# Ninety-five of 174 tensor subtractions of a transformer block go from the vector engine to GpSimd

## The chip, the core and the metric

The kernel runs on one core of a Trainium2 chip. The core's engines run side by side, each through its own fixed queue of instructions: PE multiplies matrices, DVE does element-wise work and reductions, ACT does activations and casts, POOL is GpSimd, and SP issues the DMAs. An instruction waits only for semaphores of instructions that it depends on. The metric is the device time of one execution in microseconds (us); the median of three runs of the kernel before is 856.67 us (856.55 to 857.07).

## The reference

One pre-norm transformer block in float32 on 2048 tokens of width 640. Attention is local and dilated: each token sees itself and the 7 tokens at distances 2, 4, ... 14 before it, in 32 heads of width 20. The feed-forward part is a SwiGLU of width 1728.

```python
def _A_ref(x, wqkv, wo):          # H=32, Dh=20, W=8, dil=2
    idx = pos[:, None] - (arange(W) * dil)[None, :]
    logits = einsum("bhsd,bhswd->bhsw", q, kg) * Dh ** -0.5
    logits = where(idx >= 0, logits, -1e9)
    o = einsum("bhsw,bhswd->bhsd", softmax(logits, -1), vg)
    return o.reshape(B, S, D) @ wo
def _B_ref(x, w_gate, w_up, w_down):
    return (silu(x @ w_gate) * (x @ w_up)) @ w_down
h = x + _A_ref(layernorm(x), A_wqkv, A_wo)
h2 = h + _B_ref(layernorm(h), B_w_gate, B_w_up, B_w_down)
```

## The kernel before

**High and low halves.** PE multiplies a rounded format (fp32r) at one pass. To keep float32 accuracy, every operand is split: ACT casts it to fp32r (the high half), DVE subtracts that from the float32 value (the low half), and PE makes three passes: high by high, low by high, high by low. So each weight tile, each layer-norm output, each attention output and each gated activation costs one cast on ACT and one subtraction on DVE. The sites of these subtractions are L438 (turned layer-norm columns), L508 (Q, K and V weights), L669 (output weights), L714 (attention output), L788 (feed-forward weights) and L842 (gated activations).

**Stages.** The tokens go in four blocks of 512 (b = 0 to 3), the heads in four groups of eight (g). L536 makes Q, K and V of a block and group in 15 matmuls per bank; ACT evicts them (L543) and SP writes them to DRAM. Attention has no matmul: for each of the 16 pairs (b, g), DVE multiplies Q with the windows of K (L600, two halves of 2560 elements a partition), sums over the 20 channels (L605), takes the maximum over the 8 keys and subtracts it (L616, L617); ACT takes the exponential (L618); DVE sums, inverts and scales (L624 to L626), multiplies with V (L631), adds the eight keys in three steps (L640) and transposes (L647). SP stores the result (L653). When all four groups of a block have stored one half, SP loads it as columns (L709), ACT and DVE split it (L713, L714), and PE multiplies with the output weights (L724; for the last block L1054). Then follow layer norm and 14 feed-forward tiles: gate and up (L812), silu on ACT (L847), the product on DVE (L848), its split (L841, L842), and down (L827, L977). L392 and L481 are transposes of layer-norm output on PE, and L395 and L396 split what they give. The feed-forward weights of block 0 are split and saved (L803), and blocks 1 and 2 load most of them back (L798).

**Order.** Nothing is scheduled on the chip. Every step is registered with its engine, its reads and its writes (`P.add`), and `ORDER`, a table of numbers written into the kernel, says for each engine in which order its steps are emitted. PE, DVE, ACT and SP work through that order, and a step that is late holds up all that stand behind it on its engine. In the kernel before, POOL has only memsets and the making of an identity matrix. The costs that `P.add` is given play no part on the chip.

Of the kernel before, what the change touches and what calls it, by code (L numbers as in the profile page):

```python
# [8 lines left out]
F32 = mybir.dt.float32  # L9
# [17 lines left out]
QUEUES = (0, 1) * 8  # L27
TURN1, TURN2 = (2,), (2,3)
# [141 lines left out]


def dve(n):
    return 0.155 + 0.00104 * n


tt = dve


def nb(chunks, size):
    return (chunks / 16 * 0.042 + chunks * size / 435e3) * RATE  # L180


# [4 lines left out]
def program(tc, x_in, wqkv_in, wo_in, ffn_in, ffl_in, const_in, out):  # L187
    nc = tc.nc
    V, A, T, Q, G = nc.vector, nc.scalar, nc.tensor, nc.sync, nc.gpsimd
    P = Plan()  # L190
# [1092 lines left out]
```

## Time and profile before

| | |
|---|---|
| median of three runs | 856.67 us (856.55 to 857.07) |
| profiled execution, its own time | 859.16 us |
| its span | 857.4 us |
| PE busy | 845.8 us (99%), 3977 matmuls |
| DVE busy | 696.7 us (81%), 807 instructions |
| ACT busy | 412.3 us (48%), 722 instructions |
| POOL busy | 3.3 us, 12 instructions |
| DMA moved | 177.75 MB, mean 207 GB/s |
| granted clock of PE, mean | 0.998 |

The page's busy tenths show DVE at nine tenths or more from the third of 40 slices to the twenty-eighth (one of them at eight), about 43 to 600 us: attention runs there from about 60 us on. PE is busy all through, because the feed-forward work of one block is interleaved with the attention of the next. The busy time of PE hides gaps of up to some 0.16 us between matmuls, since a matmul is shown longer (390 ns for 512 columns) than the distance to the next one (227 ns, 20.40 us for 90 of them in the chain of waits).

### The profile page before, as it was taken

How to read it: one execution, taken by the hardware profiler on the slowest of the kernel's cores; microseconds unless marked ns; L12 is line 12 of the kernel's file. 1: busy time of each engine (PE TensorE's matmuls, PEld its weight loads, DVE VectorE, ACT ScalarE, POOL GpSimd, SP SyncE). 2: the span in 40 equal slices, each digit the busy share in tenths (PEclk: the TensorE clock that was granted, in tenths of full speed). 3: DMA queues.
4: the chain of work that ended last, by engine and by line, in shares of the span. 5: the costliest groups of instructions: out<-in, count | busy, mean ns of one | idle time of the engine just before them, and what ended most of it. 6: DMA issues, size and time to landing. Idle time of an engine off the chain costs nothing.

```text
span 857.4 us, 10685 instructions
## 1 busy us (share of the span) xinstructions
PE 845.8 (99%) x3977; PEld 718.0 (84%) x3977; DVE 696.7 (81%) x807; ACT 412.3 (48%) x722; POOL 3.3 (0%) x12
## 2 busy tenths in 40 slices
PE   7999999999989999999999999999999999999998
PEld 6888888889978888888888888778888888888886
DVE  5499999999999999998999999999666865553333
ACT  6766555342783434576343458454356423232332
POOL 0000000000000000000000000000000000000000
PEclk9999999999999999999999999999999999999999
DMA  5997795779798889648989987887653213362312
GB/s 185 277 262 180 231 280 137 210 200 239 218 266 269 278 271 278 215 118 293 318 269 285 306 263 200 246 305 274 251 172 101 98 53 99 97 216 100 107 31 93
DMA packets 86852, 177.75 MB, mean 207 GB/s; under 512 B 33408, under 2 KB 51584, under 8 KB 86032
## 3 DMA queue, kind: packets, MB, share of 16 engines
q1 hardware_dynamic: 85392, 176.41, 67.2%
q10 hardware_dynamic: 1408, 0.66, 0.3%
q8 instruction: 31, 0.51, 0.2%
q14 instruction: 21, 0.17, 0.1%
HBM read 132.07 MB, written 43.65 MB: 205 GB/s over the span
## 4 chain that ended last, share of the span: by engine, by line
PE 97%; ACT 1%; DVE 1%; DMA 1%; issue 0%; SPq 0%; ACTq 0%; DVEq 0%
PE bank L812 35%; PE bank L536 24%; PE bank L827 21%; PE bank L977 7%; PE bank L724 6%; PE bank L1054 2%; PE bank L392 1%; DMA fa<-in_x_dram 1%; PE bank L481 0%; PE bank L1161 0%; ACT L847 0%; ACT L618 0%; ACT ra L793 0%; ACT shb L395 0%; DVE fa L352 0%
## 5 line engine op out<-in xcount | busy, mean ns | idle before, releaser
L812 PE MATMUL bank<-shb,ra 128*128 128x512 f32 x1050 | 251.8, 390 | 1.7 <-ACT shb L395 1.2
L812 PEld LDWEIGHTS bank<-shb,ra 128*128 128x128 f32 x1050 | 196.2, 188 | 43.3 <-ACT shb L395 1.4
L827 PE MATMUL bank<-ra,acts 128*128 128x512 f32 x656 | 170.4, 391 | 0.0
L827 PEld LDWEIGHTS bank<-ra,acts 128*128 128x128 f32 x656 | 122.0, 188 | 24.1
L536 PE MATMUL bank<-ra,sha 128*128 128x512 f32 (+2 forms) x480 | 108.3, 384 | 0.3 <-ACT sha L483 0.3
L536 PE MATMUL bank<-ra,shb 128*128 128x512 f32 (+1 forms) x470 | 102.7, 378 | 0.0
L536 PEld LDWEIGHTS bank<-ra,sha 128*128 128x128 f32 x480 | 90.6, 190 | 13.8 <-ACT sha L483 0.6
L536 PEld LDWEIGHTS bank<-ra,shb 128*128 128x128 f32 x470 | 88.0, 188 | 12.6
L600 DVE TENSOR_TENSOR pq<-kv,pq 128x2560 f32<-128x2560 f32 x32 | 90.2, 2820 | 2.6 <-DMA kv<-ksc 2.2
L640 DVE TENSOR_TENSOR pq<-pq 128x1280 f32<-128x1280 f32 (+2 forms) x96 | 89.7, 934 | 2.3
L631 DVE TENSOR_TENSOR pq<-kv,pq 128x2560 f32<-128x2560 f32 x32 | 90.3, 2823 | 0.9
L605 DVE TENSOR_REDUCE pq<-pq 128x128 f32<-128x2560 f32 x32 | 90.0, 2812 | 0.4
L788 DVE TENSOR_TENSOR ra<-fa,ra 128x640 fp32r<-128x640 f32 x70 | 56.3, 819 | 26.6 <-ACT ra L778 23.7
L543 ACT ACTIVATE st<-bank,fa 128x480 f32<-128x480 f32 (+3 forms) x120 | 50.6, 474 | 55.7 <-PE bank L536 41.4
L778 ACT CAST ra<-fa 128x640 fp32r<-128x640 f32 x56 | 40.6, 727 | 57.0 <-PE bank L827 56.2
L841 ACT CAST acts<-fa 128x512 fp32r<-128x512 f32 x52 | 32.1, 620 | 61.1 <-DVE fa L848 45.5
L793 ACT CAST ra<-fa 128x1280 fp32r<-128x1280 f32 (+1 forms) x41 | 50.0, 1220 | 23.5 <-PE bank L812 17.6
L724 PE MATMUL bank<-ra 128*128 128x320 f32 x360 | 56.3, 309 | 0.0
L724 PEld LDWEIGHTS bank<-ra 128*128 128x128 f32 x360 | 54.3, 188 | 1.9 <-ACT fa L727 0.5
L848 DVE TENSOR_TENSOR fa<-bank,fa 128x512 f32<-128x512 f32 x42 | 28.8, 686 | 28.7 <-PE bank L812 19.8
L847 ACT ACTIVATE fa<-bank 128x512 f32<-128x512 f32 x42 | 25.1, 597 | 55.1 <-PE bank L812 53.2
L827 PE MATMUL bank<-acts,ra 128*128 128x512 f32 x164 | 45.3, 391 | 0.1
(161 smaller groups left out, 871.5 us busy)
## 6 DMA issues: line engine op xcount, KB each, us to landing
fa<-in_ffn_dram SPq DMA_DIRECT2D x47, 960.0 KB, 6.6
kv<-ksc SPq DMA_DIRECT2D x32, 440.0 KB, 6.0
kv<-vsc SPq DMA_DIRECT2D x32, 440.0 KB, 6.8
ra<-lsc SPq DMA_DIRECT2D x21, 640.0 KB, 6.0
lsc<-ra SPq DMA_DIRECT2D x13, 640.0 KB, 6.5
ra<-lsc SPq DMA_DIRECT2D x23, 320.0 KB, 5.2
ksc<-st SPq DMA_DIRECT2D x32, 160.0 KB, 3.9
pq<-qsc SPq DMA_DIRECT2D x16, 320.0 KB, 5.6
```

The lines of the kernel that those rows point to most:

```text
L536: T.matmul(banks[bk][:, 0:n], l, r_(wq(g, w, c) + shift, n), start=(p, c) == first_mm, stop=(p, c) == last_mm)
L543: P.add("ACT", act(m) + 0.06, lambda: A.activation(stage_t()[:, o : o + NJ * m].rearrange("p (t j c) -> p t j c", j=NJ, c=w)[:, :, j, :], ...
L600: P.add("DVE", dve(2560), lambda: V.tensor_tensor(pq(PROD, 2560).rearrange("p (j w c) -> p j w c", j=2, w=W), window(ko, 2 * jp), pq(qo + ...
L605: P.add("DVE", dve(2560), lambda: V.tensor_reduce(pq(lo + 128 * jp, 128), pq(PROD, 2560).rearrange("p (n d) -> p n d", d=DH), axis=AX.X, o ...
L631: V.tensor_tensor(pq(PROD, 2560).rearrange("p (j n d) -> p j n d", j=2, d=DH), bass.AP(tensor=v.tensor, offset=v.offset, ap=[list(v.ap[0]) ...
L640: V.tensor_add(dst(v), v[:, :, 0:m, :], v[:, :, m : 2 * m, :])
L724: T.matmul(banks[bk][:, 0:320], l, r_(m, 320), start=p == 0 and c == 0, stop=p == 2 and c == NC - 1)
L788: P.add("DVE", tt(640), lambda o=o: V.tensor_sub(ws(t, lo + o, 640)[p0:], fa[p0:, raw + o : raw + o + 640], ws(t, hi + o, 640)[p0:].bitcas ...
L793: P.add("ACT", act(n), lambda: A.copy(ws(wt, gu, n), f(raw, n)), r=[rf(raw, n)], w=[rws(wt, gu, n)], prio=PR["fh"])
L812: T.matmul(banks[bk], ws(wt, gu + 1280 * w + wid * c + col, 128), x(a, c), start=p == 0 and c == 0, stop=p == 2 and c == NC - 1)
L827: T.matmul(banks[k], l, m, start=first and p == 0, stop=stop and p == len(passes) - 1)
L977: T.matmul(banks[bk], ws(wt, o + 2048 * w + 128 * k, 128), xv_[k](a), start=first and p == 0 and k == 0, stop=stop and p == 2 and k == n - ...
```

## The change

It has four parts. A helper `low` numbers the subtractions at the sites above, and those of the attention maxima (L617), in the order in which the program registers them; those whose number is in `POOLED` go to POOL, the others stay on DVE. The activations' subtractions of blocks 2 and 3 (L842) keep DVE in any case. The logits of a group are laid out by head, row and key, where they were by row, key and head, so the maximum and the sum read eight neighbours. The normalised weights are written into the buffer of the queries, in the layout that the product with V reads. And the order of all engines is a new table. A placeholder that belonged to POOL belongs to SP now; the cost figures given to `P.add` for PE and the reciprocal also differ.

```diff
+POOLED = (1, 2, 3, 7, 9, 10, 12, 14, 18, 19, ... 161, 162, 164, 166, 167, 170)
 ORDER = {
     "PE": (
-        (0, 4), 10, 5, 4, (11, 6), (25, 2), (17, 3), (27, 8), 6, (20, 2), (35, 2), ...
+        0, 9, 1, (10, 2), 5, (2, 3), 6, (12, 3), (25, 2), 8, 7, 27, (15, 7), ...
...
+def pool(n):
+    return 0.2 + 0.00218 * n
...
+        def low(n, fn, r, w, prio):
+            k = lows[0]
+            lows[0] += 1
+            if k in POOLED:
+                P.add("POOL", pool(n), lambda: fn(G), r=r, w=w, prio=prio)
+            else:
+                P.add("DVE", dve(n), lambda: fn(V), r=r, w=w, prio=prio)
...
             P.add("DVE", dve(2560), lambda: V.tensor_reduce(
-                pq(lo + 128 * jp, 128), pq(PROD, 2560).rearrange("p (n d) -> p n d", d=DH), axis=AX.X, op=ALU.add),
+                logits(lo)[:, :, 16 * jp : 16 * jp + 16].rearrange("p h n -> p n h"), pq(PROD, 2560).rearrange("p (n h d) -> p n h d", h=8, d=DH), axis=AX.X, op=ALU.add),
...
-            P.add("DVE", dve(256), lambda: V.tensor_sub(lg, lg, mx[:, :, None, :].to_broadcast([128, NJ, W, 8])), ...
+            low(256, lambda E: E.tensor_sub(groups(lo), groups(lo), each(mo)), [rpq(lo, 256), rpq(mo, 32)], [rpq(lo, 256)], 20)
...
-            P.add("DVE", dve(256), lambda: V.tensor_mul(lg, lg, sm[:, :, None, :].to_broadcast([128, NJ, W, 8])), ...
+            P.add("DVE", dve(256), lambda: V.tensor_mul(
+                pq(qo, 256).rearrange("p (j w h) -> p h j w", j=NJ, w=W), pq(lo, 256).rearrange("p (h j w) -> p h j w", j=NJ, w=W),
+                pq(mo + 32, 32).rearrange("p (h j) -> p h j", j=NJ)[:, :, :, None].to_broadcast([128, 8, NJ, W])),
...
-                P.add("DVE", tt(640), lambda o=o: V.tensor_sub(ws(t, lo + o, 640)[p0:], ...
+                low(640, lambda E, o=o: E.tensor_sub(ws(t, lo + o, 640)[p0:], ...
```

The 95 that POOL takes are, by elements of a partition: 46 of 640, 29 of 512, 7 of 480 or 448, and 13 of 256, among these the maxima of 8 of the 16 groups. No other instruction is added or removed but one activation-table load on ACT fewer (33 to 32); PE has the same matmuls.

Three places show how the order moves. The names in the rows: `ra`, `shb`, `acts` are halves for PE, `fa` holds raw float32 data, `pq` is the attention's buffer, `kv` the windows of K and V, `bank` are PSUM banks. On DVE, the last group of block 1, from the softmax's sum to the first half's transpose; before:

```order
L624 TENSOR_REDUCE pq<-pq 128x32
L625 RECIPROCAL pq<-pq 128x32
L626 TENSOR_TENSOR pq<-pq 128x256
L631 TENSOR_TENSOR pq<-kv,pq 128x2560
L848 TENSOR_TENSOR fa<-bank_75,fa 128x512
L640 TENSOR_TENSOR pq<-pq 128x2x640
L842 TENSOR_TENSOR acts<-fa,acts 128x512
L788 TENSOR_TENSOR ra<-fa,ra 128x640 x2
L640 TENSOR_TENSOR pq<-pq 128x2x320
L640 TENSOR_TENSOR pq<-pq 128x2x160
L647 STREAM_TRANSPOSE pq<-pq 128x2x5x32
```

and in the changed kernel:

```order
L640 RECIPROCAL pq<-pq 128x32
L806 TENSOR_TENSOR ra<-fa,ra 128x640
L641 TENSOR_TENSOR pq<-pq 128x8x32
L869 TENSOR_TENSOR fa<-bank_75,fa 128x512
L806 TENSOR_TENSOR ra<-fa,ra 128x640
L649 TENSOR_TENSOR pq<-kv,pq 128x2560
L658 TENSOR_TENSOR pq<-pq 128x2x640
L806 TENSOR_TENSOR ra<-fa,ra 128x640
L658 TENSOR_TENSOR pq<-pq 128x2x320
L658 TENSOR_TENSOR pq<-pq 128x2x160
L665 STREAM_TRANSPOSE pq<-pq 128x2x5x32
```

(L806 is the old L788, L869 the old L848, and so on.) Some low halves still stand between the attention's steps, but from the program's start to the first-half transpose of block 1's last group DVE now has 32 subtractions of these kinds instead of 81, to that of block 2 it has 48 instead of 126, and to that of block 3 it has 65 instead of 160.

The queue of POOL in the stretch in which block 1's attention ends, where it had nothing:

```order
L806 TENSOR_TENSOR ra<-fa,ra 128x640 x5
L861 TENSOR_TENSOR acts<-fa,acts 128x512 x2
L732 TENSOR_TENSOR ra<-fa,ra 128x512
L806 TENSOR_TENSOR ra<-fa,ra 128x640 x6
L732 TENSOR_TENSOR ra<-fa,ra 128x512 x2
L732 TENSOR_TENSOR ra<-fa,ra 128x256
L806 TENSOR_TENSOR ra<-fa,ra 128x640 x4
```

Four of block 1's six low halves of the attention output (L732, the old L714) stand here, among 17 subtractions of the feed-forward part; the two others stayed on DVE.

On PE, the end of the Q, K and V matmuls, where the feed-forward part begins; before:

```order
L392 MATMUL bank_76<-fa 128x128 x4
L392 MATMUL bank_75<-fa 128x128 x4
L392 MATMUL bank_74<-fa 128x128 x4
L536 MATMUL bank_73<-ra,shb 128x512 x15
L536 MATMUL bank_72<-ra 128x448 x5
L536 MATMUL bank_72<-ra,shb 128x448 x5
L536 MATMUL bank_72<-ra 128x448 x5
L392 MATMUL bank_76<-fa 128x128 x4
L392 MATMUL bank_75<-fa 128x128 x4
L812 MATMUL bank_74<-shb,ra 128x512 x5
```

and in the changed kernel:

```order
L546 MATMUL bank_71<-ra,shb 128x448 x15
L403 MATMUL bank_75<-fa 128x128 x4
L403 MATMUL bank_74<-fa 128x128 x4
L403 MATMUL bank_76<-fa 128x128 x4
L546 MATMUL bank_72<-ra 128x448 x5
L546 MATMUL bank_72<-ra,shb 128x448 x5
L546 MATMUL bank_72<-ra 128x448 x5
L403 MATMUL bank_75<-fa 128x128 x4
L830 MATMUL bank_74<-shb,ra 128x512 x15
```

One group of four transposes, not two, stands between the last Q, K and V matmul and the first feed-forward matmul. Further on, the first matmul with the output weights has 1573 matmuls ahead of it for block 1 before and 1502 now (71 of 512 columns fewer), 2273 and 2213 for block 2, 2730 and 2725 for block 3.

More of the change, by code (lines that the diff above doesn't have):

```diff
@@ L609, in att_exp, with groups, each @@
+        def groups(lo):
+            return pq(lo, 256).rearrange("p (n w) -> p n w", w=W)
+        def each(o):
+            return pq(o, 32)[:, :, None].to_broadcast([128, 32, W])
         def att_exp(b, g, n, ko, vo, qo, lo, mo):
[L610 removed]
             if b == 0:
                 P.add("DVE", dve(256), lambda: V.tensor_add(
[L613 removed]
+                    logits(lo), logits(lo), f(MASK, 32)[:, None, :].to_broadcast([128, 8, 32])),
@@ L841, in act_split @@
             P.add("ACT", act(512), lambda: A.copy(o(0), i()), r=[srcr], w=[("ab", ao, ao + 512)], prio=0)
-            P.add("DVE", dve(512), lambda: V.tensor_sub(o(1), i(), o(0).bitcast(F32)), r=[srcr, ("ab", ao, ao + 512)], w=[("ab", ao + 512, ao + 1024)], prio=0)
+            if b < 2:
+                low(512, lambda E: E.tensor_sub(o(1), i(), o(0).bitcast(F32)), [srcr, ("ab", ao, ao + 512)], [("ab", ao + 512, ao + 1024)], 0)
+            else:
+                P.add("DVE", dve(512), lambda: V.tensor_sub(o(1), i(), o(0).bitcast(F32)), r=[srcr, ("ab", ao, ao + 512)], w=[("ab", ao + 512, ao + 1024)], prio=0)
         def gate_up(b, i, wt, gu, ao, so, first):
@@ L1113, in wo3 @@
                     apply(j)
-            P.add("POOL", 0.02, lambda: None, w=[("fakv0", 0, KV_N), ("fakv1", 0, KV_N), ("xh", 0, 2560)] + [(f"xk{fq}", 0, 2560) for fq in range(4)], prio=0)
+            P.add("SP", 0.02, lambda: None, w=[("fakv0", 0, KV_N), ("fakv1", 0, KV_N), ("xh", 0, 2560)] + [(f"xk{fq}", 0, 2560) for fq in range(4)], prio=0)
             for n in range(16):
```

42 lines of the change are left out of this document (19 added, 23 removed), and 156 rows, old and new, of the table ORDER.

## The prediction

> **What bounds the kernel now.** I read the shares of the engines, the chain of waits, the waits of PE, then the stretch of attention by windows and by lines. The page's engine row and its chain:
>
> ```profile
> span 857.4 us, 10685 instructions
> PE 845.8 (99%) x3977; PEld 718.0 (84%) x3977; DVE 696.7 (81%) x807; ACT 412.3 (48%) x722; POOL 3.3 (0%) x12
> ...
> PE 97%; ACT 1%; DVE 1%; DMA 1%; issue 0%; SPq 0%; ACTq 0%; DVEq 0%
> ```
>
> PE carries 97% of the chain, so an edit on DVE and POOL can win only what PE waits, and can lose without limit. What PE waits for (engine and line, waited for: us in total, times, longest):
>
> ```profile
> PE bank L481 <- DVE sha L484: 2.1, 1, 2.1
> PE bank L407 <- POOL ra L1185: 1.4, 1, 1.4
> PE bank L812 <- ACT shb L395: 1.2, 1, 1.2
> PE bank L481 <- DVE fa L354: 0.9, 1, 0.9
> PE bank L392 <- DVE shb L396: 0.7, 1, 0.7
> PE bank L536 <- ACT ra L529: 0.6, 1, 0.6
> PE bank L812 <- ACT fa L847: 0.5, 1, 0.5
> PE bank L536 <- ACT sha L483: 0.3, 1, 0.3
> ```
>
> These sum to 7.7 us, all in eight single waits. The first, second, fourth and eighth belong to the start (4.7 us); 0.6, 0.7 and 1.2 us are the seam from Q, K and V to the feed-forward part. DVE is the engine that is nearly a second bound, in one stretch (us; PE, PEld, DVE, ACT, POOL busy with counts; clock, DMA share, GB/s):
>
> ```profile
> 200.00:600.00 400.00, 396.87 (x1905) 336.88 (x1904) 380.65 (x396) 204.70 (x323) 0.73 (x2) 1.00 0.84 259
> ```
>
> DVE is busy 380.65 of 400 us and idle 19.35; PE is idle 3.13. So PE's order already lives with a DVE that is 95% full. Whether the change helps hangs on what DVE's load becomes there, and on how much of the relief PE's new order has spent in advance.
>
> **The change part by part.** *What DVE gives up.* The same stretch by lines on DVE (line, operation, tiles, shapes, count | busy us, mean ns | idle before):
>
> ```profile
> L631 DVE TENSOR_TENSOR pq<-kv,pq 128x2560 f32<-128x2560 f32 x22 | 62.1, 2822 | 0.5
> L640 DVE TENSOR_TENSOR pq<-pq 128x1280 f32<-128x1280 f32 (+2 forms) x66 | 61.6, 934 | 1.5
> L600 DVE TENSOR_TENSOR pq<-kv,pq 128x2560 f32<-128x2560 f32 x21 | 59.2, 2821 | 2.5 <-DMA kv<-ksc 2.2
> L605 DVE TENSOR_REDUCE pq<-pq 128x128 f32<-128x2560 f32 x21 | 59.0, 2811 | 0.2
> L788 DVE TENSOR_TENSOR ra<-fa,ra 128x640 fp32r<-128x640 f32 (+1 forms) x41 | 32.7, 817 | 0.0
> L848 DVE TENSOR_TENSOR fa<-bank,fa 128x512 f32<-128x512 f32 x29 | 19.8, 684 | 5.3 <-PE bank L812 4.3 <-ACT fa L847 1.0
> L842 DVE TENSOR_TENSOR acts<-fa,acts 128x512 fp32r<-128x512 f32 x28 | 19.0, 677 | 1.0 <-ACT acts L841 1.0
> L714 DVE TENSOR_TENSOR ra<-fa,ra 128x512 fp32r<-128x512 f32 (+1 forms) x15 | 8.6, 594 | 0.0
> L616 DVE TENSOR_REDUCE pq<-pq 128x32 f32<-128x256 f32 x11 | 7.1, 646 | 0.2
> L624 DVE TENSOR_REDUCE pq<-pq 128x32 f32<-128x256 f32 x11 | 7.0, 640 | 1.7 <-ACT pq L618 1.7
> ```
>
> By the order, POOL's 27th to 76th subtractions (from the first feed-forward weights to the last maximum) fall in about this stretch: 25 of 640 elements, 19 of 512 and 6 of 256. On DVE they cost 25 x 0.82 + 19 x 0.68 + 6 x 0.42 = 35.9 us (the last from the row of the subtraction of the maxima, below). The 10 before that in the start replace 6.6 us in a DVE that waits for weights there, and the 19 after it stand where DVE has room (39.07 us busy of 60 from 600 on, and less later), so I put both at nothing; their cover is work that PE has in front of these passes, and without it each of 640 elements is about 0.7 us later (1.51 less 0.82).
>
> ```profile
> 600.00:660.00 60.00, 60.00 (x291) 51.18 (x290) 39.07 (x81) 30.96 (x52) 0.00 (x0) 1.00 0.55 187
> ...
> L617 DVE TENSOR_TENSOR pq<-pq 128x256 f32<-128x256 f32 x16 | 6.8, 423 | 0.3
> L1191 POOL TENSOR_SCALAR_AFFINE_SELECT fa<-fa 128x128 f32<-128x128 f32 x1 | 0.3, 292 | 0.1
> L1190 POOL MEMSET fa<- 128x128 f32 x1 | 0.2, 204 | 0.0
> L1185 POOL MEMSET ra<- 128x512 f32 x1 | 0.5, 524 | 0.3 <-POOLq L1272 0.3
> L783 POOL MEMSET ra<- 64x640 f32 x3 | 1.9, 627 | 192.2 <-PE bank L827 192.2
> ```
>
> *What POOL then needs.* No row has a subtraction on POOL. The two memsets give a pass of (524 - 204) / 384 = 0.83 ns an element and 97 ns fixed; the select, which reads one operand besides writing, takes 88 ns more for 128 elements, 0.69 ns an element. Two operands and a result make 2.21 ns an element: 1.51 us for 640, 1.23 for 512, 0.66 for 256. Ends: the bare memset's 0.63 us for 640, and three full passes, 1.70. I take 1.51, which follows the row with an operand. The 50 then keep POOL busy 25 x 1.51 + 19 x 1.23 + 6 x 0.66 = 65 us (28 to 73), far from full. The Trainium skill (GPSIMD Engine Reference, section 3.1, Elementwise) has 4497 ns for a two-input add of 2048 elements; in proportion that is 1.41 us for 640, an estimate, and the 50 would take 60 us.
>
> *The maximum and the sum on eight neighbours.* L616 and L624 take 646 and 640 ns where a subtraction of the same 256 elements takes 423, and L605, which reads neighbours, takes no longer than L600. If the stride of eight is the reason, 22 of them save up to 22 x 0.22 = 4.8 us; if not, nothing. I take half, 2.4. The strided writes of the logits and of the normalised weights I put at nothing: L842 and L788 write and read in plain order at the same rate as everything else, and no row shows a write with a stride at a price; if it has one, DVE is that much later, under the range's upper end.
>
> *What POOL does to DVE.* This term decides. While POOL reads two operands and writes, DVE's own instructions may be held up. In this trace POOL never reads beside a busy DVE, so the price lies between nothing and POOL's whole 65 us. Of DVE's 380.65 us, 62.1 + 61.6 + 59.2 + 32.7 + 19.0 + 8.6 = 243 (64%) go to instructions with two operands from SBUF, which have most to share; the sums of L605, 2.81 us each and behind each L600, read one. A POOL subtraction that runs beside a sum costs nothing even then. I take half, 32.5 us.
>
> The stretch's DVE load is then 380.65 - 35.9 - 2.4 + 32.5 = 374.9 us: six less than before, not forty less.
>
> *What PE's order asks.* Times of the chain from attention to output weights, block 1 and block 2 (start us, duration, engine, line):
>
> ```profile
> 309.60 0.51 DVE L647 STREAM_TRANSPOSE pq<-pq 128x320 f32<-128x320 f32 x1
> 338.55 1.62 PE L724 MATMUL bank<-ra 128*128 128x320 f32 x10
> ...
> 462.30 0.51 DVE L647 STREAM_TRANSPOSE pq<-pq 128x320 f32<-128x320 f32 x1
> 467.91 0.97 SPq L709 DMA_DIRECT2D fa<-osc  x2
> 474.66 0.62 ACT L713 CAST ra<-fa 128x512 fp32r<-128x512 f32 x1 [1.69 <-DMA fa<-osc]
> 481.26 1.29 DVE L714 TENSOR_TENSOR ra<-fa,ra 128x512 fp32r<-128x512 f32 x2
> 485.25 1.92 PE L724 MATMUL bank<-ra 128*128 128x320 f32 x12
> ...
> 828.67 20.40 PE bank L827 x90
> ```
>
> From the half's transpose to the first matmul with the output weights PE leaves 338.55 - 310.11 = 28.4 us in block 1 and 485.25 - 462.81 = 22.4 in block 2. The new order puts 71 and 60 matmuls fewer ahead of that point; at 20.40 / 90 = 0.227 us each PE gets there 16.1 and 13.6 us sooner. DVE's six us, shared over the stretch, bring its end forward by about 2 and 4. That leaves 28.4 - 16.1 + 2 = 14.3 and 22.4 - 13.6 + 4 = 12.8 us. The chain needs 5.1 from the transpose to the load's issue, 6.75 to the cast, 0.62 for it, and the subtraction, now 1.23 on POOL behind feed-forward subtractions of 1.51; with two of these in front, 16.7 us. So PE is short by 2.4 us, and at block 2 by 3.9, of which the first stop has paid 2.4: 3.9 us together.
>
> *The other terms.* The 29 products L848 stand in DVE's queue between attention's steps, and where DVE is behind PE's plan, PE's next gate and up wait for their bank: queued behind a late L600 are L848, its split, and then PE's down pass. Now PE pays 0.5 us for this; at worst each would come one DVE operation late, 29 x 0.68 = 20 us. I take 3, near the row. At the seam one group of transposes, not two, stands before the first feed-forward matmul: of 2.5 us I count 1.5 as gained. The start's 4.7 us I leave, with 2 either way. One ACT table load fewer costs and wins nothing: ACT is 48% busy.
>
> Sum: 3.9 + 3.0 - 1.5 = +5.4 us. The profiled execution took 859.16 us by its own time, 1.8 more than its span, and the median is 856.67; 5.4 on the median gives **862 us**.
>
> **The rivals.** *Nothing is held up (faster).* POOL and DVE work side by side. DVE's load falls to 342 to 345 of 400 us, its slack before the output weights grows, and PE's 3.13 us of idle in the stretch go: 853.5 us, at best 850.5 with the start's 3.0 us on DVE too. For it: POOL has 65 us of work in 400, nothing in the profile shows the two in each other's way. Against: nothing shows them apart either, and two thirds of DVE's time is of the kind that would clash.
>
> *They exclude each other.* A subtraction on POOL stops DVE for its whole length, always or when DVE's instruction has two SBUF operands. Then DVE carries 0.64 x 65 = 42 to 65 us more, 384 to 407; with some 9 us in which it waits for PE, DMA and ACT in any case (5.3, 2.5 and 1.7 in the rows), that is 393 to 416 of 400. It decides from about 30 us on, where the relief is used up; at 42 it is 9 us beyond the forecast, at 65 PE waits 16 us for the stretch and the 3 of the products: 871 to 882 us, say 876. The Trainium skill (SBUF — State Buffer, section SBUF: two separate sides) states just this: DVE and GpSimd share a pair of ports as an exclusive lock for the whole instruction, also for a DVE operation with two SBUF inputs against a GpSimd operation that reads SBUF. No run here shows it yet; by that rule the lower of the two loads, 384, is the one to expect.
>
> *Nothing changes.* PE's order absorbs both, since what DVE loses to POOL equals what it gives away, and the output weights' chain is shorter than I count: 857 us.
>
> **How the numbers follow.** Forecast 0.35 (its own range 859 to 868), exclusion 0.17, side by side 0.31, nothing changes 0.17. A difference under 0.2% (1.7 us) can't be told from none here. So faster 0.31, same 0.17, slower 0.52. The range, 852 to 884, leaves out the best of the side-by-side case and the worst of exclusion (from the 73 us end of POOL's work), less than 0.2 together.
>
> **What would show it.** Right: products of 2560 elements on DVE with means over 2.82 us, POOL subtractions near 1.5 us, DVE busy within 10 us of 375 in that stretch, and new waits of PE for POOL's L732 or DVE's L869. Products still at 2.82 us mean that the two don't meet: the prediction is wrong in its deciding term, and the time is near 853. A wait of PE at the seam as large as before takes 1.5 us off the gain. A DVE above 385 us means exclusion.

## The result: slower, 889.2 us

The changed kernel takes 889.2 us (median of four runs, 887.55 to 892.31) where the kernel before takes 856.87 (856.55 to 858.55): a ratio of 1.0377, 95% interval 1.0345 to 1.041. That is 32 us more, 27 above the forecast and 5 above the range. The sign was right, and the cause was only in part the one forecast. Three single executions of other runs that lie far out (`oldorder_writes` at 1425 us with a granted clock of 0.557, `layout_old` at 2105, the kernel before beside them at 4872) are left out of the medians and ratios below. From the page of the changed kernel (busy time by engine, chain of waits):

```profile
span 886.8 us, 10781 instructions
PE 855.5 (96%) x3977; PEld 720.6 (81%) x3977; DVE 680.1 (77%) x712; ACT 407.7 (46%) x721; POOL 172.4 (19%) x107
...
PE 54%; DVE 27%; DMA 11%; issue 3%; ACT 3%; SPq 2%; DVEq 0%
```

PE's share of the chain fell from 97% to 54%, and DVE with DMA has 38%. The chain runs through DVE's attention up to about 490 us and on PE from there. DVE's busy time fell by only 16.6 us, and POOL, shown busy for 172 us, spent part of that time waiting, as a piece of its timeline further down shows. The stretch from 200 to 600 us by windows (columns as in the prediction):

```profile
200.00:600.00 400.00, 382.10 (x1807) 321.72 (x1807) 359.51 (x318) 191.51 (x312) 107.30 (x58) 0.99 0.81 245
```

and by lines, on DVE and, the last, on POOL:

```profile
L658 DVE TENSOR_TENSOR pq<-pq 128x1280 f32<-128x1280 f32 (+2 forms) x63 | 73.0, 1158 | 1.6
L610 DVE TENSOR_TENSOR pq<-kv,pq 128x2560 f32<-128x2560 f32 x21 | 61.7, 2940 | 2.6 <-DMA kv<-ksc 2.4
L615 DVE TENSOR_REDUCE pq<-pq 128x128 f32<-128x2560 f32 x21 | 59.1, 2814 | 0.3
L869 DVE TENSOR_TENSOR fa<-bank,fa 128x512 f32<-128x512 f32 x26 | 17.8, 683 | 15.5 <-PE bank L830 12.4 <-ACT fa L868 3.1
...
L806 POOL TENSOR_TENSOR ra<-fa,ra 128x640 fp32r<-128x640 f32 (+1 forms) x25 | 51.1, 2051 | 60.5 <-ACT ra L811 33.9 <-ACT ra L796 19.6 <-PE bank L845 3.3
```

L658 (the old L640) went from a mean of 934 to 1158 ns. L615 with one operand and L869 with one from PSUM stayed where they were. DVE is idle 40.5 us of 400, not 19.35, and PE 17.9, not 3.1. PE's largest waits are ones that were small or absent before: for DVE's products (L869), for the halves of the layer norm at the seam between blocks 0 and 1 (L407, the old L396, 0.7 us before), for activations. None is for POOL's L732. The five largest in the changed kernel (us in total, times, longest):

```profile
PE bank L830 <- DVE fa L869: 5.4, 6, 1.4
PE bank L403 <- DVE shb L407: 4.3, 2, 3.8
PE bank L845 <- DVE acts L861: 2.3, 1, 2.3
PE bank L845 <- ACT acts L859: 2.2, 1, 2.2
PE bank L742 <- ACT fa L745: 2.1, 2, 1.3
```

**Where the time goes.** Two points cut the loss into pieces in each block: the transposes of blocks 1 and 2 from which the prediction counted, and PE's first matmuls with the output weights behind them. In the changed kernel (start us, duration):

```profile
319.90 0.52 DVE L665 STREAM_TRANSPOSE pq<-pq 128x320 f32<-128x320 f32 x1
339.23 2.06 PE L742 MATMUL bank<-ra 128*128 128x320 f32 x13
...
474.45 0.50 DVE L665 STREAM_TRANSPOSE pq<-pq 128x320 f32<-128x320 f32 x1
501.49 2.36 PE L742 MATMUL bank<-ra 128*128 128x320 f32 x15
```

PE reaches block 2's output weights 501.49 - 485.25 = 16.2 us later than before, with 13.6 us less work done on the way: 29.8 us lost, and the two profiled executions differ by 888.54 - 859.16 = 29.4. So nothing of note is lost behind that point. DVE's transposes come 10.3 and 12.2 us later than before. What DVE did up to block 1's transpose, before and after (DVE's busy time is 278.96 and 271.68 us):

```profile
0.00:309.60 309.60, 302.42 (x1446) 261.76 (x1447) 278.96 (x298) 170.69 (x353) 1.27 (x8) 0.99 0.80 233
```

```profile
0.00:319.90 319.90, 302.74 (x1424) 260.14 (x1425) 271.68 (x257) 165.78 (x349) 67.89 (x48) 0.98 0.77 218
```

Busy 7.3 us less, idle 48.2 us in place of 30.6. **Up to that point the relief is small, as forecast (7.3 us here, six in the forecast's stretch), and DVE idles 17.6 us more.** The experiments had to explain both halves: why the relief is so small, and where the idle time comes from.

### The profile page after: what moved, and what is told of

Read it like the earlier page. It is cut to its first block, busy times and chain, and to the rows that moved or that the text cites. A ratio compares the mean times of both kernels' runs of the same rounds, so it can differ in the third digit from the quotient of the medians.

```text
span 886.8 us, 10781 instructions
## 1 busy us (share of the span) xinstructions
PE 855.5 (96%) x3977; PEld 720.6 (81%) x3977; DVE 680.1 (77%) x712; ACT 407.7 (46%) x721; POOL 172.4 (19%) x107
## 4 chain that ended last, share of the span: by engine, by line
PE 54%; DVE 27%; DMA 11%; issue 3%; ACT 3%; SPq 2%; DVEq 0%
PE bank L830 22%; PE bank L845 16%; PE bank L998 7%; DVE pq L649 6%; DVE pq L658 6%; DVE pq L610 4%; PE bank L546 3%; DVE pq L615 3%; DMA kv<-ksc 3%; PE bank L742 3%; PE bank L1075 2%; DMA fa<-in_ffn_dram 2%; DMA lsc<-ra 2%; DMA fa<-osc 1%; DMA kv<-vsc 1%
## 5 line engine op out<-in xcount | busy, mean ns | idle before, releaser
L830 PE MATMUL bank<-shb,ra 128*128 128x512 f32 x1050 | 255.0, 394 | 6.9 <-DVE fa L869 5.4
L845 PE MATMUL bank<-ra,acts 128*128 128x512 f32 x656 | 168.4, 392 | 0.4 <-POOL acts L861 0.3
L658 DVE TENSOR_TENSOR pq<-pq 128x1280 f32<-128x1280 f32 (+2 forms) x96 | 108.8, 1134 | 2.5
L806 POOL TENSOR_TENSOR ra<-fa,ra 128x640 fp32r<-128x640 f32 (+1 forms) x38 | 72.4, 1916 | 159.0 <-ACT ra L796 79.4
L610 DVE TENSOR_TENSOR pq<-kv,pq 128x2560 f32<-128x2560 f32 x32 | 92.7, 2898 | 7.2 <-DMA kv<-ksc 4.5
L649 DVE TENSOR_TENSOR pq<-kv,pq 128x2560 f32<-128x2560 f32 x32 | 92.1, 2879 | 0.9
L615 DVE TENSOR_REDUCE pq<-pq 128x128 f32<-128x2560 f32 x32 | 90.1, 2815 | 0.6
L869 DVE TENSOR_TENSOR fa<-bank,fa 128x512 f32<-128x512 f32 x42 | 28.8, 685 | 65.4 <-PE bank L830 51.4
L796 ACT CAST ra<-fa 128x640 fp32r<-128x640 f32 x56 | 40.5, 726 | 50.7 <-PE bank L845 50.6
```

The lines of the kernel that those rows point to most:

```text
L610: P.add("DVE", dve(2560), lambda: V.tensor_tensor(pq(PROD, 2560).rearrange("p (j w c) -> p j w c", j=2, w=W), window(ko, 2 * jp), pq(qo + ...
L615: P.add("DVE", dve(2560), lambda: V.tensor_reduce(logits(lo)[:, :, 16 * jp : 16 * jp + 16].rearrange("p h n -> p n h"), pq(PROD, 2560).rea ...
L649: V.tensor_tensor(pq(PROD, 2560).rearrange("p (j n d) -> p j n d", j=2, d=DH), bass.AP(tensor=v.tensor, offset=v.offset, ap=[list(v.ap[0]) ...
L658: V.tensor_add(dst(v), v[:, :, 0:m, :], v[:, :, m : 2 * m, :])
L806: low(640, lambda E, o=o: E.tensor_sub(ws(t, lo + o, 640)[p0:], fa[p0:, raw + o : raw + o + 640], ws(t, hi + o, 640)[p0:].bitcast(F32)), [ ...
L830: T.matmul(banks[bk], ws(wt, gu + 1280 * w + wid * c + col, 128), x(a, c), start=p == 0 and c == 0, stop=p == 2 and c == NC - 1)
```

## The experiments

Ratios are against the kernel before, run beside each; differences in us between kernels that were run at different times are good to about 2 us (the kernel before had medians from 856.87 to 858.67). Line numbers shift with the edits; the tiles tell which line is which.

**First: POOL or the order?** In the expectations three theories stand against each other: A, by which POOL's disturbance of DVE is the price; B, by which the changed order is; and C, by which POOL is merely slower and its low halves come late. `neworder_dve` has the changed order and layout, and every subtraction back on DVE, at the place where POOL had begun it:

```diff
-POOLED = (1, 2, 3, 7, 9, 10, 12, 14, ... 167, 170)
+POOLED = ()
 ORDER = {
     "DVE": (the 95 inserted by POOL's starting times)
```

> The changed kernel with all 95 subtractions back on DVE, each standing in DVE's queue where POOL began it; PE, ACT and SP keep the new order, the logits the new layout. Theory A (a POOL subtraction and a DVE instruction with two SBUF operands exclude each other for their whole length): the products of 2560, the sums of 1280, 640 and 320 elements are back at 2.82, 1.49, 0.82 and 0.49 us; DVE has the 66 us of subtractions back but not the 46 us of stretching; time 858 to 870. Theory B (the new order costs the time, whoever subtracts): 880 to 900. Theory C (POOL's subtractions are only slower, 1.57 against 0.82 us, and come late for PE): 855 to 862.

Measured: 888.13 us, 1.0341 (1.0322 to 1.036): B's number, the changed kernel's time with no subtraction on POOL. Its DVE is undisturbed and carries the full load:

```profile
PE 856.5 (97%) x3977; PEld 721.8 (81%) x3977; DVE 691.8 (78%) x807; ACT 407.4 (46%) x721; POOL 3.2 (0%) x12
...
L669 DVE TENSOR_TENSOR pq<-pq 128x1280 f32<-128x1280 f32 (+2 forms) x96 | 89.7, 934 | 2.0
```

`oldorder_pool` is the reverse, before's layout and order with the same 95 subtractions on POOL:

```diff
+POOLED = (15, 17, 20, 68, 73, 77, ...)
+        if n in POOLED:
+            eng = "POOL"
```

> The kernel before, its layout and its order of PE, ACT and SP, with the same 95 subtractions on POOL, in the order in which DVE began them. Theory A: DVE's two-operand instructions are stretched by 40 to 50 us in all, like in the changed kernel, and the time goes up to 862 to 885. Theory B: within 2 us of 857. Theory C: no stretching on DVE, new waits of PE for POOL, 858 to 868.

Measured: 863.04 us, 1.0051 (1.0035 to 1.0067). DVE's instructions are stretched as in the changed kernel, which C had not, and relief and stretching together cost 4.6 us: the low end of what A had, and more than B's 2:

```profile
PE 91%; DVE 3%; DMA 2%; ACT 1%; issue 1%; POOL 1%; SPq 1%; ACTq 0%; DVEq 0%; POOLq 0%
...
L655 DVE TENSOR_TENSOR pq<-pq 128x1280 f32<-128x1280 f32 (+2 forms) x96 | 107.4, 1119 | 2.4
```

`pool_writes` is the changed kernel, but POOL fills each tile and reads only one element. The 95 low halves and maxima are left out of the result.

```diff
+    def tensor_sub(self, out, a, b):
+        one = (slice(None),) + (slice(0, 1),) * (len(out.shape) - 1)
+        self.g.tensor_sub(out[one], a[one], b[one])
+        for _ in range(3):
+            self.g.memset(out.bitcast(F32), 0.0)
```

> The changed kernel in which POOL leaves the subtraction out: for each of the 95 it subtracts one element (so it waits for the same things) and then writes the whole tile three times without reading (3 x 0.63 us for 640 elements, longer than the 1.57 us of an undisturbed subtraction). Theory A, with the exclusion tied to reading SBUF: DVE's two-operand instructions are back at 2.82, 1.49, 0.82, 0.49 us but for the short subtractions, and the time is 852 to 862. Theory B: 880 to 895. Theory C: 885 to 900, since POOL is busy longer than before.

Measured: 865.4 us (860.34 to 871.73), 1.0103 (1.0059 to 1.0146). POOL is busy longer (214.6 us), DVE is undisturbed, and 23 us of the loss are gone, which B and C, with 880 or more, had not; but the kernel isn't faster than before, and its median is over A's 862 (the page below is of the fastest execution, 860.34):

```profile
PE 846.8 (99%) x3977; PEld 717.9 (84%) x3977; DVE 634.9 (74%) x712; ACT 408.3 (48%) x721; POOL 214.6 (25%) x392
...
L669 DVE TENSOR_TENSOR pq<-pq 128x1280 f32<-128x1280 f32 (+2 forms) x96 | 89.7, 935 | 2.5
```

`pool_outside` leaves POOL only the 27 subtractions that begin before 60 or after 600 us:

```diff
-POOLED = (1, 2, 3, ... 18, 19, 22, 23, ... 129, 133, 137, ... 170)
+POOLED = (1, 2, 3, 7, 9, 10, 12, 14, 18, 19, 137, 140, ... 170)
```

> The changed kernel with the 27 subtractions on POOL that begin in the first 60 us or after 600 us of the profile; the 68 between, where attention runs, are on DVE as in the run with none on POOL. Theory A: the stretching goes to under 6 us, and the time is within 4 us of the run with none on POOL. Theory B: 880 to 900. Theory C: within 4 us of the run with none on POOL too, since the late ones have slack.

Measured: 887.83 us, 1.034 (1.0317 to 1.0364), the time with none on POOL, which all three theories allow. The 27 outside bring and cost nothing, so what matters lies in the 68 between.

What follows: A and B are each half of it, and C is out. DVE's busy time by the page is 691.8 us with all on DVE, 634.9 when POOL only writes, and 680.1 in the changed kernel. Of 56.9 us of relief, the disturbance takes 45.2 back. The new order with that load costs what it costs with no relief at all. In the old order the whole move costs 4.6 us, relief and disturbance together, and the new order with full relief (865) is no better than the old order without any (858).

**How POOL holds DVE up.** A piece of the changed kernel, DVE's rows of its timeline and then POOL's (start us, duration):

```profile
301.88 2.81 DVE L615 TENSOR_REDUCE pq<-pq 128x128 f32<-128x2560 f32 x1
...
308.40 2.82 DVE L649 TENSOR_TENSOR pq<-kv,pq 128x2560 f32<-128x2560 f32 x1
311.25 2.46 DVE L658 TENSOR_TENSOR pq<-pq 128x1280 f32<-128x1280 f32 x1
313.63 2.19 DVE L806 TENSOR_TENSOR ra<-fa,ra 128x640 fp32r<-128x640 f32 x1
```

```profile
302.75 1.57 POOL L806 TENSOR_TENSOR ra<-fa,ra 128x640 fp32r<-128x640 f32 x1
308.48 3.88 POOL L861 TENSOR_TENSOR acts<-fa,acts 128x512 fp32r<-128x512 f32 x1 [4.16 <-ACT acts L859]
312.32 4.94 POOL L806 TENSOR_TENSOR ra<-fa,ra 128x640 fp32r<-128x640 f32 x2
```

The first POOL row lay beside DVE's sum of 301.88 to 304.69 us, which reads one operand, and took 1.57 us. The second came 0.08 us after DVE's product L649. It ended at 312.36, only some 1.1 us after that product's end at 311.22; meanwhile L658, alone 1.5 us for 1280 elements, took 2.46. The product that began first wasn't stretched, though POOL's instruction lay beside it for 2.7 us. This holds over the whole trace: of DVE's 78 instructions with two SBUF operands that meet a subtraction of POOL (a 79th, counted below, meets only a fill), 26 began first and last what they last alone (mean excess -1 ns, at most 9), and 52 found POOL's running and last 883 ns longer on the mean, none under 197. So the two take turns whole instruction by whole instruction, and the wait is inside the busy time of both. `pool_one_read` has POOL copy the first operand (one read; the low halves are left out again):

```diff
-            self.g.memset(out.bitcast(F32), 0.0)
+        self.g.tensor_copy(out, a)
```

> The changed kernel, but POOL copies the first operand into the low half instead of subtracting (one operand read from SBUF, and a one-element subtraction; the 95 low halves are left out). Theory X1 (any reading of SBUF by POOL and DVE's reading of two operands exclude each other): DVE's instructions with two SBUF operands that overlap a copy are stretched by 300 to 700 ns each, and the time is 872 to 890. Theory X2 (only two reads on both sides exclude): means of DVE as undisturbed (2.82, 1.49, 0.82, 0.49), the time 860 to 868 as with writes alone.

Measured: 867.81 us, 1.0105 (1.007 to 1.014), with DVE's means slightly over the undisturbed ones:

```profile
L668 DVE TENSOR_TENSOR pq<-pq 128x1280 f32<-128x1280 f32 (+2 forms) x96 | 93.1, 970 | 2.5
L659 DVE TENSOR_TENSOR pq<-kv,pq 128x2560 f32<-128x2560 f32 x32 | 91.5, 2859 | 0.9
```

Sorted by whether they overlap a data instruction of POOL, DVE's instructions with two SBUF operands last, against 155 ns + 1.04 ns an element (the means of the undisturbed ones, by size, lie within 12 ns of that, but for the strided write of L641; worked out from all rows of the traces):

```
kernel          POOL does          overlapping   mean excess   sum
after           subtracts (2 in)        79          581 ns    45.9 us
oldorder_pool   subtracts (2 in)        76          586 ns    44.5 us
pool_one_read   copies (1 in)           88          132 ns    11.7 us
pool_writes     fills (0 in)           113           10 ns     1.2 us
after, DVE instruction with a PSUM operand   17      -4 ns
after, DVE reduction (one operand)           24      -5 ns
```

Reading is what excludes, also with one operand: X1 in kind. The copy of 640 elements needs 0.72 us alone and not 1.57, so it holds DVE for less. The 300 to 700 ns expected by X1 were too much, X2's undisturbed means are missed too (2859 and 970 ns for 2823 and 934), and the time, 867.81, is in X2's range and not in X1's. The rule of the Trainium skill (SBUF — State Buffer, section "Who interferes with whom"), a lock held for the whole instruction between DVE with two SBUF inputs and a GpSimd instruction that reads SBUF, not one that only writes, agrees with every row of this table.

**Second: why the order needs the relief.** The theories: D, the price sits at one place, the seam between blocks 0 and 1; E, DVE's load as such, paid wherever the relief is missing. `relief_early` gives POOL, as fills, the 18 dense subtractions before 262 us, `relief_late` the 50 from there to 600; the other subtractions are on DVE, and the filled low halves are left out.

```diff
-POOLED = (1, 2, 3, ...)
+POOLED = (the 18)           # relief_late: (the 50)
-                P.add("POOL", pool(n), lambda: fn(G), ...)
+                P.add("POOL", pool(n), lambda: fn(Writes(G)), ...)
```

> The changed order and layout; of the 68 subtractions that the change gives to POOL between 60 and 600 us, the 18 before 262 us (before the seam between blocks 0 and 1 is over) go to POOL, which only writes there (one-element subtraction and three fills of the tile: these 18 low halves are left out), the other 77 of the 95 stay on DVE. So DVE is truly relieved up to the seam and not after it. Theory D (the price sits at the seam, where PE waits 12.5 us and its clock halves): nearly all of the 23 us between 888 (no relief) and 865 (full relief) comes back, 865 to 872. Theory E (PE's new order asks for the relief everywhere, and each part that is missing is paid where it is missing): a share, 876 to 884; replaying the queues with the durations of the trace of the kernel with all on DVE gives 880.

> The complement: the 50 subtractions from 262 to 600 us go to POOL as writes only (left out), the 18 before and the 27 outside stay on DVE. D: the seam is unrepaired, 880 or more. E: the other share, 870 to 880 (the same replay gives 876); the gains of the two halves together are about the whole 23 us.

Measured: 876.88 us, 1.0226 (1.0185 to 1.0266), and 874.6, 1.019 (1.0166 to 1.0214). Both are in E's ranges and outside D's. The gains, 11.3 and 13.5 us from 888.1, add up to 24.8, about the 22.7 of the full relief. But the 18 take 8.4 us from DVE's busy time (691.8 to 683.4 by the pages) and the 50 take 29.6 (to 662.2), and they buy nearly as much, so the early part has something of its own. The seam in the changed kernel (from its timeline, start us, duration, engine, line, and what ended the wait):

```profile
253.67 1.26 ACT L811 CAST ra<-fa 128x1280 fp32r<-128x1280 f32 x1 [6.36 <-DMA fa<-in_ffn_dram]
...
254.84 1.07 ACT L406 CAST shb<-bank 128x512 fp32r<-128x512 f32 x2
...
255.45 0.69 DVE L407 TENSOR_TENSOR shb<-bank,shb 128x512 fp32r<-128x512 f32 x1 [6.04 <-ACT shb L406]
...
256.19 0.66 PE L403 MATMUL bank<-fa 128*128 128x128 f32 x4 [3.80 <-DVE shb L407]
```

ACT waits 6.36 us for a load of feed-forward weights, and the cast that PE needs stands behind it in ACT's queue. SP issued that load and the one before it at

```profile
231.71 0.58 SPq L792 DMA_DIRECT2D fa<-in_ffn_dram  x1
238.23 0.58 SPq L792 DMA_DIRECT2D fa<-in_ffn_dram  x1
```

though their buffers were free at 186.8 and 199.0 us (the ends of the last work on them in the trace): in SP's table they now stand behind loads of attention that wait for DVE's products. The kernel before issues these two at

```profile
205.44 0.58 SPq L774 DMA_DIRECT2D fa<-in_ffn_dram  x1
213.66 0.45 SPq L774 DMA_DIRECT2D fa<-in_ffn_dram  x1
```

`loads_forward` moves these two entries, numbers 347 and 350, and nothing else:

```diff
     "SP": (
-        ... 100, 336, 97, 95, 99, 103, 179, ... 200, 202, 350, 190, 201, 195, 203, 347, 196, ...
+        ... 100, 336, 97, 95, 99, 350, 347, 103, 179, ... 200, 202, 190, 201, 195, 203, 196, ...
```

> The changed kernel with two entries of SP's order moved: the first two loads of feed-forward weights behind the seam, whose buffers are free at 186.8 and 199.0 us but which stand in SP's queue behind attention's loads and are issued at 231.7 and 238.2, go 16 places and 21 places ahead, to about 214 us (before issues its own at 205 and 214). Theory Q (SP's queue is a large part: the weights late, DVE's subtraction of them waits 5 us, PE behind it, then PE's clock halves): 5 to 12 us less than the changed kernel's 889, 877 to 884. Theory E (DVE is the chain there and takes up the waiting with other work): 884 to 889; the replay gives 4 us less.

Measured: 882.04 us, 1.0267 (1.0242 to 1.0291), 7.2 us less than the changed kernel (about 9 by the two ratios). The seam by windows, changed kernel first:

```profile
240.00:280.00 40.00, 34.92 (x154) 28.64 (x153) 27.91 (x32) 22.50 (x38) 8.52 (x7) 0.91 0.86 227
```

```profile
240.00:280.00 40.00, 39.55 (x186) 33.14 (x185) 35.09 (x39) 22.04 (x35) 9.35 (x7) 1.00 0.77 231
```

PE does 186 matmuls there and not 154, DVE is busy 35.09 us and not 27.91, and the clock stays whole: theory Q. `relief_late_loads` joins the same move to `relief_late`:

```diff
 relief_late, and in "SP":
-        ... 200, 202, 350, 190, 201, 195, 203, 347, 196, ...
+        ... 99, 350, 347, 103, ... 200, 202, 190, 201, 195, 203, 196, ...
```

> relief_late (the 50 subtractions from 262 to 600 us taken from DVE and only written by POOL, so left out; 45 on DVE) with the two loads of feed-forward weights moved ahead in SP's order as in loads_forward. Theory Q (what the relief before the seam bought is that these two loads are in time; the place in SP's queue is the price there): 865 to 869, as with the relief everywhere (865). Theory E (DVE's load before the seam has its own price beside them): 870 to 875, at most a few us below relief_late's 874.6.

Measured: 868.57 us, 1.012 (1.0091 to 1.0149), Q's number, 6 us under `relief_late` and 3 above full relief (within their spread). So most of what the early relief bought, some 6 of 9 us, was these two loads in time.

**Third: what the order's other queues have to do with it.** `dve_act_resorted` keeps the changed order on PE, SP and POOL, all subtractions on DVE, and sorts DVE's and ACT's whole queues anew by readiness; `layout_old_order` does so on all five engines, with before's starts as the rank. Both change only `ORDER`.

```diff
 ORDER = {
-    "DVE": (as in neworder_dve), "ACT": (as in the changed kernel)
+    "DVE", "ACT": (of what is ready, what came first before)      # layout_old_order: all five
```

> The changed layout and PE's, SP's and POOL's changed order, all subtractions on DVE as in neworder_dve; but DVE's and ACT's queues are sorted anew: whenever the engine comes free it takes, of what is ready, what came first in the kernel before. So no ready work stands behind work that isn't. D' (the price is the fixed order of DVE's and ACT's queues, in which PE's food stands behind late work): back to 858 to 868. E (PE's own order asks too early, and DVE hasn't the time): only a part comes back, 870 to 880; replaying the queues with the traced durations gives 874.

> The changed layout (logits by head, weights into the queries' buffer), every subtraction on DVE, and on all five engines the order of before, as far as it is ready (the queries' buffer is now held until the weighted sum, so its loads come later). E and D: the layout alone costs nothing, DVE's load falls by about 2.4 us in the dense stretch; 852 to 858. Rival L (the layout is part of the price: the strided write of the multiplication, the queries' load that comes later): 862 to 875.

Measured: 903.4 us, 1.0526 (1.0502 to 1.0551), and 906.0, 1.0548 (1.0501 to 1.0596): both worse than any other kernel and outside every range expected, the first 29 us over the 874 of the replay, the second 48 over the 858 of D and E; the replay took the DMAs' landing times of another trace as fixed. In `layout_old_order` the products with K wait 12.3 us for their loads, before 2.2. They tell nothing about the theories. Two gentler kernels took their place. `fed_first` moves 50 of DVE's steps:

```diff
 ORDER = {
-    "DVE": (as in neworder_dve)
+    "DVE": (50 steps that PE soon consumes, moved ahead to where their operands are ready)
```

> neworder_dve with one queue changed a little: of DVE's 730 steps, the 50 that PE consumes within 2 us of their end and that had their operands over 0.3 us before they began (evictions and low halves, 179 us of standing in the queue in all) go ahead to where their operands are ready; nothing else moves. Theory D' (PE's food stands in DVE's queue behind attention and weight subtractions, and that is the price): 865 to 880. Theory E (what they pass is needed a little later, and DVE has no time to spare): 884 to 892; the replay of the queues gives 888.

Measured: 885.44 us, 1.0329 (1.0283 to 1.0375), against 888.13 for `neworder_dve`: the intervals overlap, and it is E's number. So D' is out as far as a small reordering of DVE can show it: PE's food doesn't merely stand in a wrong place in DVE's queue. `layout_old` has before's own order on PE, ACT and DVE with the changed layout:

```diff
 the changed kernel's layout, POOLED = (), before's ORDER;
 in "SP" the sixteen loads pq<-qsc go behind the weighted sum that frees their buffer
```

> The changed layout alone, with every subtraction on DVE and before's own order on PE, ACT and DVE word for word (layout_old_order had sorted all five queues anew and so told nothing of the layout). On SP only the sixteen loads of queries move: their buffer now holds the normalised weights until the weighted sum has read them, so each load goes where its buffer is free. Theory E (the layout is no part of the price): 854 to 860. Rival L (the later loads of queries make DVE wait for its first product of a window, about 6 us of landing at some windows): 862 to 870; a replay of the queues with the traced durations gives 866 where it gives 859 for before.

Measured: 859.51 us, 1.001 (0.9989 to 1.0031): the layout costs nothing that can be told, E. `oldorder_writes` is `oldorder_pool` with fills in place of subtractions (left out again):

```diff
-            Either.on = G if n in POOLED else nc.vector
+            Either.on = Writes(G) if n in POOLED else nc.vector
```

> Before's order and layout, the same 95 subtractions taken from DVE, but POOL only writes (one-element subtraction and three fills of the tile: the 95 low halves are left out), so DVE is relieved of about 66 us and nothing disturbs it. Theory E (in the old order PE sets the end and DVE's time is worth nothing, the relief can only be spent by another order): 852 to 859, within 1% of before. Rival R (DVE's load is on the path in the old order too): 835 to 850.

> oldorder_writes again, since its profiled execution ran at a TensorE clock of 0.557 and can't be read (95 low halves left out). E as before: within 1% of before, 852 to 866, PE's waits for DVE small and DVE idle over 100 us more than before. R: 835 to 850. If it is 865 or more again: the fills by POOL have a price of their own of some us, which pool_writes and both relief runs then hold too.

Measured: 869.12 us, 1.0112 (1.0068 to 1.0157), and the same kernel again, as `oldorder_writes2`, 871.48 us, 1.0154 (1.0124 to 1.0184). Relief without disturbance makes the old order slower, not faster, so R is out, and E's number was missed too. PE's waits in `oldorder_writes2` say where:

```profile
PE bank L838 <- ACT fa L873: 6.1, 2, 5.4
PE bank L750 <- POOL ra L188: 2.7, 2, 2.1
```

The one of 5.4 us is at 324 to 330 us, and the chain there is the seam's over again: POOL's fill is late, SP's store of it waits, the next weight load behind it in SP's queue lands 10 us after its issue at 317.9, and ACT's cast of it stands ahead of the silu that PE needs. I placed POOL's entries by the times at which DVE had done them; another placing may be better. So whether the fills have a price of their own isn't settled; if they have, `pool_writes` and the relief kernels hold it too, and true relief is worth more than their times show.

## Why the prediction was right and wrong

**Right in size, by luck: what POOL does to DVE.** The deciding term of the forecast was half of POOL's time, 32.5 us in the stretch. Measured from the rows between 200 and 600 us, 54 of DVE's two-operand instructions overlap POOL and are 31.1 us longer. But the half was a middle between nothing and all, with no mechanism behind it; the mechanism at work is the one of the rival that had 0.17. POOL's subtraction was put at 1.51 us for 640 elements; alone it takes 1.57. Sums and PSUM operands are untouched, as the prediction had it. What it left out is the rest of the program: 25 more such overlaps outside the stretch, 14.8 us. Exclusion's own price of 42 to 65 us for the stretch was too high: there 19 of the overlaps fall on sums and 10 on PSUM operands, which aren't held up, and where DVE began first it is POOL that waits. Of the signs named, the slower products and the waits for L869 came; POOL near 1.5 us holds only where it is alone (the mean of L806 in the stretch is 2051 ns), and DVE's busy time there, 359.51 us, is 15 below the forecast's 375: DVE idles 40.5 us, which the forecast hadn't seen.

**Right in part: the layout.** L633 and L639 take 415 and 409 ns where L616 and L624 took 646 and 640: the stride was the reason, and 22 of them save 5.1 us. The strided write of the weights, put at nothing, costs: L641 took 424 ns before, as L626, and 658 in `neworder_dve`, where nothing disturbs it. Eleven of these in the stretch give back 2.6. The 2.5 that are left are the forecast's 2.4, by luck: the saving was twice that, and the write's price took half of it. `layout_old` shows that neither matters for the time.

**Wrong: "What PE's order asks".** The forecast brought DVE's transposes of blocks 1 and 2 forward by 2 and 4 us, by spreading six us of lower load, and so found PE short by 3.9 us in front of the output weights, waiting for POOL's L732. Measured, they come 10.3 and 12.2 us later, and PE loses 29.8 us on the way to block 2's output weights; the profile shows no wait for L732, as PE is held up before it gets there, at the seam for the layer norm's halves (L407) and in many places for the products (L869). The load did fall (by 7.3 us up to block 1), but DVE's idle time, which the step took as given, rose by 17.6 us. Where, by windows of 0 to 60, 60 to 240 and 240 to 280 us; before, then after (its third window, with DVE busy 27.91 us, is shown at the seam above):

```profile
0.00:60.00 60.00, 55.32 (x255) 47.01 (x256) 39.07 (x65) 42.97 (x91) 1.17 (x7) 0.97 0.81 242
60.00:240.00 180.00, 180.00 (x895) 159.57 (x893) 173.10 (x159) 93.96 (x217) 0.00 (x0) 1.00 0.77 212
240.00:280.00 40.00, 37.50 (x169) 30.69 (x168) 38.98 (x51) 21.10 (x30) 0.10 (x1) 1.00 0.90 273
```

```profile
0.00:60.00 60.00, 54.04 (x240) 45.01 (x241) 30.94 (x43) 38.61 (x85) 14.46 (x17) 0.94 0.78 226
60.00:240.00 180.00, 175.30 (x867) 154.94 (x866) 174.05 (x155) 90.20 (x210) 26.25 (x15) 1.00 0.73 204
```

Between 60 and 240 us DVE is full in both, so what it misses on either side it never makes up. It idles 8.1 us more in the start, where the prediction left "2 either way", and 11.1 us more at the seam, where it counted 1.5 us as gained. The lower load isn't what makes it idle: in the same order with every subtraction on DVE, `neworder_dve`, it idles as long, 321.61 - 273.61 = 48.0 us. With the two loads moved, `loads_forward`, it idles 310.90 - 271.40 = 39.5 at the load of the changed kernel. The windows of the two up to the transpose:

```profile
0.00:321.61 321.61, 303.38 (x1424) 259.86 (x1425) 273.61 (x296) 165.70 (x349) 1.27 (x8) 0.97 0.76 217
```

```profile
0.00:310.90 310.90, 299.84 (x1424) 257.63 (x1425) 271.40 (x257) 165.71 (x349) 67.10 (x48) 0.99 0.78 224
```

In `loads_forward` the transpose is back within 1.3 us of before's 309.60, and yet PE reaches block 2's output weights at 494.21 us, 9.0 later than before with 13.6 us less work on the way: 22.6 us are lost still. In this order PE has to be there sooner than before, and for that a transpose as early as before's isn't early enough. What it needs, `pool_writes` shows. Its window up to the transpose, and PE's first matmul behind it from its timeline:

```profile
0.00:299.15 299.15, 292.96 (x1402) 253.49 (x1403) 251.79 (x256) 163.98 (x347) 79.37 (x155) 0.99 0.81 231
```

```profile
321.99 2.36 PE L753 MATMUL bank<-ra 128*128 128x320 f32 x15
```

With true relief the transpose comes 10.4 us sooner than before, though DVE idles 47.4 us, and PE is at block 1's output weights at 321.99 us, 16.6 sooner, as the 71 matmuls fewer said (16.1). The count of the order was right; it is an order for a DVE with some 27 us less to do by then, and it got 7.

**Wrong: "the other terms".** With the products at 3 us and the seam at -1.5 they were to come to 1.5. The seam, counted as a gain, costs 7 to 9 us by `loads_forward` and 6.0 by `relief_late_loads`. PE's waits for L869 are 5.4 us in six, not 3; those for activations, 4.5 us more. Why two weight loads would be late could be read before the run: they are entries of SP's table that moved behind attention's loads. I compared the tables of DVE and PE at this place and not SP's.

**What stays open.** The 8.1 us in the start aren't traced further than DVE's waits for ACT's casts of the first weights, nor shown to cost that much at the end: `pool_writes`, at 865, idles 31.9 us there, more than the changed kernel's 29.1. Of the 16 us or so between 882 and 865, about 13 come back with the relief behind the seam (`loads_forward` to `relief_late_loads`); they go in many small waits, which no single move was shown to mend. No version tried beats the kernel before.

## What to carry to other kernels

Work that is moved to an engine which shares a path with the loaded one should be counted after what the sharing takes back: here 45 of 57 us, because the moved work reads two operands while DVE's own instructions do; a copy took back 12 and a fill 1. An order that has been fitted to a relief pays for each part of it that doesn't come, so time the order with the old assignment, and the assignment in the old order, before both together. Where a fixed order is new, compare every queue's table, the DMA issuer's first: a load that went behind a wait is a stall which no busy share shows.

## What the hardware did that I had not expected

- POOL's instruction waits for DVE's as well: it takes up to 4.15 us in place of 1.57 for 640 elements, and a one-element subtraction up to 2.84 us in `pool_writes` where most take 0.19. The profile shows all of it as busy time.
- After the stall at the seam (waits of 3.80 and 1.13 us) PE's clock was granted at half for some 5 us:

```profile
254.00:258.00 4.00, 0.68 (x5) 0.47 (x5) 2.55 (x4) 4.00 (x8) 2.94 (x2) 0.87 0.81 231
258.00:262.00 4.00, 4.00 (x10) 3.17 (x11) 4.00 (x4) 3.97 (x8) 0.64 (x1) 0.50 0.85 220
```

  Twelve matmuls of 512 columns in a row, from 258.54 to 263.66 us, began 427 ns apart and not 227, so a stall of 5 us cost 2.4 more. The Trainium skill (TensorE: Matmul & The Clock Gate, section "What's actually happening") has the clock halved after a window of about 3.4 us without work, which agrees with this row.
- A stride of eight float32 elements costs DVE as much in a write (424 to 658 ns for 256 elements) as in a reduction's reads (415 to 646).
